# Second stage: another order for the work before the first scores, one output column and one product of v exchanged, two output columns begun in the tail

## The chip, the cores and the metric

The kernel runs on one core of a Trainium2 chip. The metric is the device time of one execution in microseconds; the number of the kernel before is the median of three runs.

## The reference

Three layers in a row on 8 batches of 576 tokens and 512 features (8 heads of 64): attention with keys and values averaged in groups of 8, a gated MLP with a product over the tokens, and a layer of four experts. The second stage of the kernel is the last one:

```python
logits = x @ w_gate
topk = np.argpartition(-logits, K, axis=-1)[..., :K]      # K = 2
...
for e in range(E):                                        # E = 4
    q = x @ wq[e]
    k = x @ wk[e]
    v = x @ wv[e]
    scores = scale * (q @ k.transpose(0, 2, 1))
    scores = np.where(causal, -1000000000.0, scores)
    scores = scores - scores.max(-1, keepdims=True)
    a = np.exp(scores)
    a /= a.sum(-1, keepdims=True) + 1e-09
    ye = a @ v @ wo[e]
    for kk in range(K):
        mask = topk[:, :, kk] == e
        out += mask[..., None] * w[:, :, kk:kk + 1] * ye
```

## The kernel before

The first stage (attention and MLP, until about 589 us) writes its result to DRAM as two parts, a high one of TensorE's precision and the remainder. Class PhaseB is the second stage. Every product of fp32 accuracy is made of three matmuls on such parts: high by high, high by low, low by high.

The four experts are two pairs p. For a batch b and a pair p there are nine units u, each a tile of scores: QT lists them as (row of 128 tokens i, expert of the pair e), and e = 2 is the last 64 tokens of both experts together. The main loop in run goes over all 8 x 2 x 9 units in this order, and in its step k issues:

- score of unit k: matmuls on TensorE (PE, L827 to L840), mask and maximum on VectorE (DVE, L832, L834, L841), the exponential on ScalarE (ACT, L844);
- scale of unit k - 1: sum and reciprocal on DVE (L855, L856), the scaling of the probabilities pr on GpSimd (POOL, L860), or on DVE for the units in SDF (batch 0) and SDL (last batch);
- the fill items of that step (below);
- after units 5 and 8, av: the product of probabilities and v of one expert (PE L906, ACT L910, DVE L911, then the parts ah and al, ACT L916 and DVE L917);
- trans of unit k - 3 (LAG): the transposes of pr (PE L873, L886) and their two parts pbh and pbl (ACT L877, L890, DVE L882, L891).

So the order of each engine's work is the order in which the program issues it, and the tables of fill items set where the rest goes. An item of two characters is: xN, load chunk N of the next batch's input; 1N, part N of the projections of this batch's pair 1 (0 and 1 are q's halves, 2 and 3 k's halves, 12 matmuls each); 0N, the same of the next batch's pair 0; vN, product of v for the next batch, tokens N; g, the next batch's gates; oN, output column N of the batch before (12 matmuls L928 to L930, two evictions on ACT L931, one transfer L932). FIRSTF, FILL and LASTF are the tables of batch 0, of batches 1 to 6 and of the last one; PRE is issued ahead of the first unit, for batch 0 itself.

A half of k is copied on ACT (L744, tile scr), its remainder taken on DVE (L745), and after the second half four transfers spread it (kd, L751, on SP's queue). q goes the same way (ACT L726, L728, L734, DVE L729, L731, two transfers qz, L737). v is copied at L785. All products go through a ring of 8 PSUM banks (bank); outp's tile o has 3 buffers. The last batch's output columns come behind the main loop, which runs LAG + 1 = 4 steps past the last unit.

Of the kernel before, what the change touches and what calls it, by code (L numbers as in the profile page):

```python
# [8 lines left out]
F32 = mybir.dt.float32  # L9
# [7 lines left out]
B, H, S, D = 8, 8, 576, 64  # L17
# [24 lines left out]
class PhaseA:  # L42


    def __init__(self, ctx, tc, w, ins, x2d):
        self.tc, self.nc, self.ins, self.x2d = tc, tc.nc, ins, x2d
        self.c = self.w = w
        self.ps = ctx.enter_context(tc.tile_pool(name="a_ps", bufs=1, space=bass.MemoryType.PSUM))
        self.E, self.LN, self.XX, self.XU, self.GG = {}, {}, {}, {}, {}
        self.P, self.X32, self.XH, self.XL, self.U, self.G = {}, {}, {}, {}, {}, {}  # L50
        self.PT, self.VN, self.QT, self.KV, self.RAW, self.STG = {}, {}, {}, {}, {}, {}
# [396 lines left out]
    def outp(self, b, f):  # L448
        nc, w = self.nc, self.w
        ps = self.ps.tile([128, 2, 512], F32, tag="mm", name="op", bufs=2)  # L450
        c = slice(f * 128, f * 128 + 128)
        for h in range(2):
            s = slice(h * HS, h * HS + HS)
            o = ps[:, h, :HS]
            for k in range(4):
                gh, gl = self.G[b, k]
                nc.tensor.matmul(o, self.wo[0][:, k, c], gh[:, s], start=k == 0, stop=False)  # L457
                nc.tensor.matmul(o, self.wo[0][:, k, c], gl[:, s], start=False, stop=False)  # L458
                nc.tensor.matmul(o, self.wo[1][:, k, c], gh[:, s], start=False, stop=k == 3)  # L459
        hi, lo = (w.tile([128, 2, HS], F32R, tag="x2", name=n, bufs=4) for n in ("x2h", "x2l"))  # L460
        x = ps[:, :, :HS] if f < 3 else lo.bitcast(F32)
        nc.vector.tensor_add(x, ps[:, :, :HS], self.X32.pop((b, f)))
        nc.scalar.activation(hi, x, AF.Copy)  # L463
        (nc.vector if f < 3 else nc.gpsimd).tensor_sub(lo, x, hi.bitcast(F32))  # L464
        for i, t in enumerate((hi, lo)):
            nc.sync.dma_start(self.x2d[b][:, f, i], t.bitcast(F32).rearrange("p a b -> p (a b)"))

    def run(self):
        self.weight_tiles()
        for b in range(B):  # L470
            n = b + 1
            more = n < B
            if b == 0:
                self.first()
            else:
                self.middle(b)
            if n + 1 < B:
                self.load_k(n + 1)
                self.load_v(n + 1, 0)
                self.load_q(n + 1)  # L480
            ahead = 1 if b else 0
            for f in range(4):
                if more:
                    if f == 0:
                        self.finish(n, 4)
                    self.trans(n, f + ahead)
                self.outp(b, f)
            if more:
                if not ahead:
                    self.trans(n, 4)  # L490
                self.av(n, (2, "r", 0, 1, 3))
# [121 lines left out]
LAG = 3  # L613
ALV = 1
KDM = 1
FILL = (('', '12 10 11', '', '13 x0 x1 x2 x3', '', '', 'o3 o1 o0', '', ''), ('v0', 'v1 00 02', '01 o2', '03', '', '', '', 'v2 v3', 'v4 g'))
FIRSTF = (('10', '11', '12', '13 x0 x1 x2 x3', '', '', '', '', ''), ('v0 00', '', '01 02 v1', '03', '', '', '', 'v2 v3', 'v4 g'))
LASTF = (('', '10 12 11', '', '', '13', '', 'o1', '', 'o0'), ('', '', '', '', '', 'o2', '', '', 'o3'))
SDF = {(0, 0), (0, 1), (0, 5), (0, 8), (1, 0), (1, 2), (1, 7)}
SDL = {(0, 4), (0, 6), (1, 6), (1, 7)}  # L620
PRE = 'v0 00 01 02 03 v1 v2 v3 v4 g'
AVS = [(0, 256), (256, S)]


class PhaseB:


    def __init__(self, ctx, tc, w, ins, x2d, out, ident):
        self.tc, self.nc, self.ins, self.x2d, self.out, self.ident = tc, tc.nc, ins, x2d, out, ident
        self.c = self.w = w  # L630
        self.ps = ctx.enter_context(tc.tile_pool(name="b_ps", bufs=1, space=bass.MemoryType.PSUM))
        self.X, self.QK, self.V, self.GW, self.U, self.PT, self.AV, self.AH = {}, {}, {}, {}, {}, {}, {}, {}

    def load_x(self, b, kc):
        nc, w = self.nc, self.w
# [280 lines left out]
            nc.scalar.activation(ah[:, lo:up], a[:, lo:up], AF.Copy)  # L916
            (nc.vector if ALV else nc.gpsimd).tensor_sub(al[:, lo:up], a[:, lo:up], ah[:, lo:up].bitcast(F32))  # L917

    def outp(self, b, f):
        nc, w = self.nc, self.w  # L920
        c = slice(128 * f, 128 * f + 128)
        o = w.tile([128, S], F32, tag="vg", name="o", bufs=3)
        for lo, up in AVS:
            ps = self.bank("op")[:, :up - lo]
            s = slice(lo, up)
            for p in range(2):
                ah, al = self.AH[b, p]
                nc.tensor.matmul(ps, self.wo[0][:, p, c], ah[:, s], start=p == 0, stop=False)  # L928
                nc.tensor.matmul(ps, self.wo[1][:, p, c], ah[:, s], start=False, stop=False)
                nc.tensor.matmul(ps, self.wo[0][:, p, c], al[:, s], start=False, stop=p == 1)  # L930
            nc.scalar.activation(o[:, s], ps, AF.Copy)  # L931
        nc.sync.dma_start(self.out[b, :, f], o)  # L932

    def run(self):
        self.consts()
        for kc in range(4):
            self.load_x(0, kc)
        self.weights()
        part = lambda b, p: [lambda w=w, h=h: self.proj(b, w, p, h) for w in "qk" for h in range(2)]
        vpart = lambda b: [lambda t=t: self.vproj(b, t) for t in range(NT)]  # L940
        units = [(b, p, u) for b in range(B) for p in range(2) for u in range(9)]
        def item(b, x):
            if x[0] == "x":
                return [lambda: self.load_x(b + 1, int(x[1]))] if b + 1 < B else []
            if x[0] == "o":
                return [lambda: self.outp(b - 1, int(x[1]))] if b > 0 else []
            if x[0] == "1":
                return [part(b, 1)[int(x[1])]]
            if b + 1 == B:
                return []  # L950
            if x[0] == "0":
                return [part(b + 1, 0)[int(x[1])]]
            if x[0] == "v":
                return [vpart(b + 1)[int(x[1])]]
            return [lambda: self.gate(b + 1)]
        for x in PRE.split():
            for f in item(0 if x[0] == "1" else -1, x):
                f()
        for k in range(len(units) + LAG + 1):
            if k < len(units):  # L960
                b, p, u = units[k]
                self.score(b, p, u)
            if 0 <= k - 1 < len(units):
                self.scale(*units[k - 1])
            if k < len(units):
                for x in (LASTF if b + 1 == B else FILL if b else FIRSTF)[p][u].split():
                    for f in item(b, x):
                        f()
            j = k - LAG
            if 0 <= j - 1 < len(units):  # L970
                b_, p_, u_ = units[j - 1]
                if u_ in (5, 8):
                    for g in range(2):
                        self.av(b_, p_, u_ // 8, g)
            if 0 <= j < len(units):
                self.trans(*units[j])
        for f in range(4):
            self.outp(B - 1, f)


def host_b(inputs, a):
# [34 lines left out]
```

## Time and profile before

| | |
|---|---|
| time, median of 3 runs (lowest, highest) | 969.14 us (969.02, 970.92) |
| the profiled execution: time, span | 967.84 us, 966.1 us |
| mean granted clock of TensorE | 0.982 |
| busy: PE, DVE, ACT, POOL | 95%, 72%, 54%, 46% |

Times in the rows are microseconds from the start of the span. A row of the timeline is one instruction or a few of a kind: start, duration, engine, line and operation, output <- inputs, shapes, and in brackets the time for which the engine had been idle, with what the profile takes to have released it. Matmuls overlap, so their durations add up to more than the time they take; the distance of their starts tells it.

### The profile page before, as it was taken

How to read it: one execution, taken by the hardware profiler on the slowest of the kernel's cores; microseconds unless marked ns; L12 is line 12 of the kernel's file. 1: busy time of each engine (PE TensorE's matmuls, PEld its weight loads, DVE VectorE, ACT ScalarE, POOL GpSimd, SP SyncE). 2: the span in 40 equal slices, each digit the busy share in tenths (PEclk: the TensorE clock that was granted, in tenths of full speed). 3: DMA queues.
4: the chain of work that ended last, by engine and by line, in shares of the span. 5: the costliest groups of instructions: out<-in, count | busy, mean ns of one | idle time of the engine just before them, and what ended most of it. 6: DMA issues, size and time to landing. Idle time of an engine off the chain costs nothing.

```text
span 966.1 us, 18451 instructions
## 1 busy us (share of the span) xinstructions
PE 915.0 (95%) x6488; PEld 864.4 (89%) x6488; DVE 693.1 (72%) x1869; ACT 519.0 (54%) x1285; POOL 447.0 (46%) x628
## 2 busy tenths in 40 slices
PE   4887699999999999999999999899999999999997
PEld 3677689989989999899899899799999999999987
DVE  6998557757667577577576514897878796878785
ACT  3755334344343343343443433677777777777776
POOL 6545847558369368376583560113222222323221
PEclk9797899999999999999999999999999999999999
DMA  9611522312402404223126014415253534435121
GB/s 326 236 35 44 172 80 82 121 61 71 157 25 81 160 13 140 99 65 132 56 61 191 25 39 134 140 37 176 61 172 88 162 94 147 118 108 163 49 61 75
DMA packets 51644, 102.86 MB, mean 106 GB/s; under 512 B 10592, under 2 KB 16736, under 8 KB 50656
## 3 DMA queue, kind: packets, MB, share of 16 engines
q1 hardware_dynamic: 51408, 101.68, 32.9%
q8 instruction: 52, 0.85, 0.4%
q14 instruction: 40, 0.33, 0.1%
q10 hardware_dynamic: 144, 0.00, 0.0%
HBM read 59.72 MB, written 28.31 MB: 91 GB/s over the span
## 4 chain that ended last, share of the span: by engine, by line
PE 63%; DVE 20%; ACT 6%; POOL 5%; issue 3%; DMA 2%; SPq 1%; POOLq 0%; ACTq 0%; DVEq 0%
PE av L906 4%; PE op L457 4%; PE op L458 4%; PE op L459 3%; PE sp L434 3%; PE sp L432 3%; PE sp L433 3%; PE sc L224 3%; PE t L886 3%; DVE vnl L402 3%; PE pj L715 2%; PE pj L713 2%; PE pj L714 2%; DVE vnh L404 2%; DVE bs L388 2%
## 5 line engine op out<-in xcount | busy, mean ns | idle before, releaser
L860 POOL TENSOR_SCALAR pr<-pr,sm,gw 128x128 f32<-128x128 f32 (+3 forms) x119 | 72.7, 612 | 208.1 <-DVE sm L856 140.9
L844 ACT ACTIVATE pr<-s,sm 128x256 f32<-128x256 f32 (+4 forms) x160 | 83.2, 521 | 41.6 <-DVE sm L841 18.0
L432 PE MATMUL sp<-wsh,vnh 128*128 128x288 f32 x256 | 78.8, 309 | 5.0 <-ACT vnh L400 5.0
L458 PE MATMUL op<-g,woh 128*128 128x288 f32 x256 | 77.0, 301 | 6.8 <-POOL g L445 6.8
L457 PE MATMUL op<-g,woh 128*128 128x288 f32 x256 | 78.5, 309 | 0.3 <-DVE x2l L464 0.3
L416 PE MATMUL up<-x,wih 128*128 128x288 f32 x256 | 76.8, 300 | 1.5 <-ACT xu L324 1.5
L433 PE MATMUL sp<-wsh,vnl 128*128 128x288 f32 x256 | 77.0, 301 | 0.0
L434 PE MATMUL sp<-wsl,vnh 128*128 128x288 f32 x256 | 76.6, 299 | 0.0
L418 PE MATMUL up<-x,wil 128*128 128x288 f32 x256 | 75.7, 296 | 0.0
L715 PE MATMUL pj<-xbh,wql 128*128 128x288 f32 x256 | 75.5, 295 | 0.0
L713 PE MATMUL pj<-xbh,wqh 128*128 128x288 f32 x256 | 75.5, 295 | 0.0
L714 PE MATMUL pj<-xbl,wqh 128*128 128x288 f32 x256 | 75.5, 295 | 0.0
L459 PE MATMUL op<-g,wol 128*128 128x288 f32 x256 | 75.3, 299 | 0.0
L417 PE MATMUL up<-x,wih 128*128 128x288 f32 x256 | 75.1, 293 | 0.0
L841 DVE CUSTOM_DVE_ANT_0 s<-s,mk 128x512 f32<-128x512 f32 (+3 forms) x128 | 62.4, 487 | 3.5 <-PE t L886 2.9
L224 PE MATMUL sc<-kbd,qt 128*128 128x144 f32 (+1 forms) x320 | 50.8, 306 | 14.2 <-DMA qt<-q_in 8.4
L891 DVE TENSOR_TENSOR pbl<-t,pbh 128x512 fp32r<-128x512 f32 (+3 forms) x128 | 60.7, 484 | 3.4 <-ACT pbh L890 1.7
L886 PE MATMUL t<-ident,pr 128*128 128x128 f32 x320 | 57.7, 280 | 4.8 <-POOL pr L860 2.6
L224 PEld LDWEIGHTS sc<-kbd,qt 128*128 128x128 f32 (+1 forms) x320 | 44.4, 192 | 18.3 <-issue 11.1
L906 PE MATMUL av<-pbh,vt 128*128 128x320 f32 (+4 forms) x224 | 55.6, 278 | 2.4 <-ACT pbh L890 2.4
L400 ACT ACTIVATE vnh<-vg,rs 128x512 fp32r<-128x512 f32 (+1 forms) x40 | 27.3, 717 | 54.9 <-POOL rs L392 43.0
L464 POOL TENSOR_TENSOR x2l<-x2l,x2h 128x576 fp32r<-128x576 f32 x8 | 11.4, 1430 | 97.1 <-ACT x2h L463 97.1
(247 smaller groups left out, 3352.8 us busy)
## 6 DMA issues: line engine op xcount, KB each, us to landing
kraw<-k_in SPq DMA_DIRECT2D x16, 576.0 KB, 3.8
x<-x2h SPq DMA_DIRECT2D x32, 288.0 KB, 2.1
x<-x2l SPq DMA_DIRECT2D x32, 288.0 KB, 2.1
xbl<-x SPq DMA_DIRECT2D x32, 288.0 KB, 4.1
xbh<-x SPq DMA_DIRECT2D x32, 288.0 KB, 4.0
kd<-scr SPq DMA_DIRECT2D x64, 144.0 KB, 2.5
out<-o SPq DMA_DIRECT2D x32, 288.0 KB, 3.7
vraw<-v_in SPq DMA_DIRECT2D x16, 512.0 KB, 4.3
```

What stands on the lines that cost most here:

```text
L224: nc.tensor.matmul(ps[:m, p // 2, (p % 2) * 144:(p % 2) * 144 + 144], qt[:, p, o:o + m], kbd[:, p, :], start=p % 2 == 0, stop=True, skip_g ...
L432: nc.tensor.matmul(o, vh[:, k, c], self.ws[0][:, k, s], start=k == 0, stop=False)
L433: nc.tensor.matmul(o, vl[:, k, c], self.ws[0][:, k, s], start=False, stop=False)
L434: nc.tensor.matmul(o, vh[:, k, c], self.ws[1][:, k, s], start=False, stop=False)
L457: nc.tensor.matmul(o, self.wo[0][:, k, c], gh[:, s], start=k == 0, stop=False)
L458: nc.tensor.matmul(o, self.wo[0][:, k, c], gl[:, s], start=False, stop=False)
L459: nc.tensor.matmul(o, self.wo[1][:, k, c], gh[:, s], start=False, stop=k == 3)
L713: nc.tensor.matmul(ps, self.wq[0][:, kc, c], xh[:, s], start=kc == 0, stop=False)
L714: nc.tensor.matmul(ps, self.wq[0][:, kc, c], xl[:, s], start=False, stop=False)
L715: nc.tensor.matmul(ps, self.wq[1][:, kc, c], xh[:, s], start=False, stop=kc == 3)
L886: nc.tensor.transpose(ps[:, j], pt[:, 128 * j:128 * j + 128], self.ident)
L906: nc.tensor.matmul(ps[:, s - lo:], vt[:, j, 2 * p + e].rearrange("p a d -> p (a d)"), t[:, e, j * PTS + s:j * PTS + up], start=j == 0 and ...
```

## The change

Three tables and one function change. PRE issues v's products and the gates first, then k, then q, then q of pair 1 (items 10 and 11), which leaves FIRSTF; 12 goes one unit earlier there. In FILL, o0 moves from unit 6 of pair 0 to unit 0 of pair 1, v0 from unit 0 to unit 1, and 02 from unit 1 to unit 2, in front of 01. A new table TAILF issues, in the second and the fourth of the four steps behind the last unit, the first six matmuls of output columns 0 and 1 of the last batch, those of pair 0 (two banks each, kept in self.OP); the six of pair 1, the evictions and the transfer follow behind the loop.

```diff
-FILL = (('', '12 10 11', '', '13 x0 x1 x2 x3', '', '', 'o3 o1 o0', '', ''), ('v0', 'v1 00 02', '01 o2', '03', '', '', '', 'v2 v3', 'v4 g'))
-FIRSTF = (('10', '11', '12', '13 x0 x1 x2 x3', '', '', '', '', ''), ('v0 00', '', '01 02 v1', '03', '', '', '', 'v2 v3', 'v4 g'))
+FILL = (('', '12 10 11', '', '13 x0 x1 x2 x3', '', '', 'o3 o1', '', ''), ('o0', 'v0 v1 00', '02 01 o2', '03', '', '', '', 'v2 v3', 'v4 g'))
+FIRSTF = (('', '12', '', '13 x0 x1 x2 x3', '', '', '', '', ''), ('v0 00', '', '01 02 v1', '03', '', '', '', 'v2 v3', 'v4 g'))
+TAILF = ('', 'i0', '', 'i1')
...
-PRE = 'v0 00 01 02 03 v1 v2 v3 v4 g'
+PRE = 'v0 v1 v2 v3 v4 g 02 03 00 01 10 11'
...
-    def outp(self, b, f):
+    def outp(self, b, f, pair=None):
...
-        o = w.tile([128, S], F32, tag="vg", name="o", bufs=3)
-        for lo, up in AVS:
-            ps = self.bank("op")[:, :up - lo]
+        first = pair == 0
+        o = None if first else w.tile([128, S], F32, tag="vg", name="o", bufs=3)
+        for i, (lo, up) in enumerate(AVS):
+            if first or pair is None:
+                self.OP[f, i] = self.bank("op")[:, :up - lo]
+            ps = self.OP[f, i]
             s = slice(lo, up)
-            for p in range(2):
+            for p in range(2) if pair is None else (pair,):
...
+            if first:
+                continue
             nc.scalar.activation(o[:, s], ps, AF.Copy)
-        nc.sync.dma_start(self.out[b, :, f], o)
+        if not first:
+            nc.sync.dma_start(self.out[b, :, f], o)
...
+            else:
+                for x in TAILF[k - len(units)].split():
+                    self.outp(B - 1, int(x[1]), 0)
...
         for f in range(4):
-            self.outp(B - 1, f)
+            self.outp(B - 1, f, 1 if f < 2 else None)
```

How the order moves is shown at three places. The first is ACT's queue in batch 1, from unit 6 of pair 0 on; o<-op are the evictions of output columns, two for each. Before:

```order
L931 ACTIVATE o<-op 128x256
L844 ACTIVATE pr,sm<-s,sm 128x512
L931 ACTIVATE o<-op 128x320
L931 ACTIVATE o<-op 128x256
L844 ACTIVATE pr,sm<-s,sm 128x384
L931 ACTIVATE o<-op 128x320
L931 ACTIVATE o<-op 128x256
L931 ACTIVATE o<-op 128x320
L890 ACTIVATE pbh<-t 128x2x128
L890 ACTIVATE pbh<-t 128x128
L844 ACTIVATE pr,sm<-s,sm 128x256
L890 ACTIVATE pbh<-t 128x4x128
```

After the change (line numbers are up by one, in outp by six):

```order
L937 ACTIVATE o<-op 128x256
L845 ACTIVATE pr,sm<-s,sm 128x512
L937 ACTIVATE o<-op 128x320
L937 ACTIVATE o<-op 128x256
L845 ACTIVATE pr,sm<-s,sm 128x384
L937 ACTIVATE o<-op 128x320
L891 ACTIVATE pbh<-t 128x2x128
L891 ACTIVATE pbh<-t 128x128
L845 ACTIVATE pr,sm<-s,sm 128x256
L891 ACTIVATE pbh<-t 128x4x128
L845 ACTIVATE pr,sm<-s,sm 128x128
L937 ACTIVATE o<-op 128x256
```

Two of the six evictions are gone from between the exponentials, and those of o0 stand behind the units' transposes.

The second place is ACT's queue at the start of stage 2, around the first exponentials (pr,sm<-s); qs and scr are the copies of q and k. Before:

```order
L774 ACTIVATE vt_6025<-vs 128x4x64
L844 ACT_TABLE_LOAD
L844 ACTIVATE pr,sm<-s_6248,sm 128x320
L798 ACTIVATE gg<-gg 128x20
L844 ACTIVATE pr,sm<-s_6252,sm 128x256
L726 ACTIVATE qs_6011<-pj 64x288
L728 ACTIVATE qs_6011<-pj 64x288
L844 ACTIVATE pr,sm<-s,sm 128x512
```

After the change:

```order
L729 ACTIVATE qs_6011<-pj 64x224
L729 ACTIVATE qs_6011<-pj 64x64
L735 ACTIVATE qs_6011<-pj 64x64 x2
L745 ACTIVATE scr<-pj 128x288
L845 ACTIVATE pr,sm<-s,sm 128x512
L845 ACTIVATE pr,sm<-s_6288,sm 128x320
L845 ACTIVATE pr,sm<-s_6292,sm 128x256
L845 ACTIVATE pr,sm<-s,sm 128x384
```

The copies of q of pair 1 and the first of its k now stand ahead of the first exponential; before they stood between the exponentials and behind them. The table load has moved up to the gates' exponential.

The third place is PE's queue in the tail, from the end of the next to last av. Before:

```order
L906 MATMUL av<-pbh,vt_6026 128x64
L886 MATMUL t<-ident,pr 128x128 x6
L906 MATMUL av<-pbh,vt_6026 128x256
L906 MATMUL av<-pbh,vt_6026 128x320
L906 MATMUL av<-pbl,vt_6026 128x320
```

After the change:

```order
L907 MATMUL av<-pbh,vt_6026 128x64
L887 MATMUL t<-ident,pr 128x128 x3
L932 MATMUL op<-ah,wqh 128x256
L933 MATMUL op<-ah,wql 128x256
L934 MATMUL op<-al,wqh 128x256
L932 MATMUL op<-ah,wqh 128x320
L933 MATMUL op<-ah,wql 128x320
L934 MATMUL op<-al,wqh 128x320
L887 MATMUL t<-ident,pr 128x128 x3
```

The six transposes of the last three units, in one piece before, now stand in two threes, with six matmuls of an output column behind each.

## Rows read from the trace of the kernel before

**Rows 1.** The page: span, and busy time of PE and PEld among the engines.

```profile
span 966.1 us, 18451 instructions
...
PE 915.0 (95%) x6488; PEld 864.4 (89%) x6488; DVE 693.1 (72%) x1869; ACT 519.0 (54%) x1285; POOL 447.0 (46%) x628
```

**Rows 2.** Windows: stretch, length, busy PE, PEld, DVE, ACT, POOL; granted clock, DMA share, GB/s.

```profile
680.80:708.80 28.00, 27.86 (x216) 27.18 (x216) 24.84 (x100) 21.96 (x69) 7.83 (x13) 1.00 0.43 112
708.80:725.80 17.00, 17.00 (x133) 16.74 (x132) 11.60 (x46) 11.63 (x38) 4.21 (x7) 1.00 0.40 135
...
658.40:663.20 4.80, 4.80 (x38) 4.71 (x37) 4.66 (x16) 3.75 (x13) 0.45 (x1) 1.00 0.92 267
...
640.00:920.00 280.00, 278.83 (x2155) 273.60 (x2154) 227.62 (x921) 209.36 (x660) 76.00 (x119) 1.00 0.40 116
...
619.30:622.70 3.40, 3.08 (x14) 3.11 (x15) 2.12 (x12) 1.32 (x5) 1.20 (x2) 0.50 0.99 346
```

**Rows 3.** Timeline, PE, batch 1, pair 0, unit 6: output products and the transposes behind.

```profile
659.17 0.28 PE L928 MATMUL op<-ah,wqh 128*128 128x256 f32 x1
...
663.83 0.31 PE L930 MATMUL op<-al,wqh 128*128 128x320 f32 x1
...
664.43 0.27 PE L886 MATMUL t<-ident,pr 128*128 128x128 f32 x1
...
664.72 0.62 PE L886 MATMUL t<-ident,pr 128*128 128x128 f32 x4
```

**Rows 4.** Timeline there: POOL's scaling of units 4 and 5, VectorE's reciprocal, the exponential.

```profile
662.63 0.45 POOL L860 TENSOR_SCALAR pr<-pr,sm,gw 128x128 f32<-128x128 f32 x1 [4.76 <-DVE sm L856]
663.40 0.78 POOL L860 TENSOR_SCALAR pr<-pr,sm,gw 128x512 f32<-128x512 f32 x1 [0.32 <-ACT o L931]
...
663.04 0.17 DVE L856 RECIPROCAL sm<-sm 128x1 f32<-128x1 f32 x1
...
661.94 0.69 ACT L844 ACTIVATE pr<-s,sm 128x512 f32<-128x512 f32 x1 [1.05 <-DVE sm L855]
```

**Rows 5.** Timeline, the same place in batch 6: PE's transposes of unit 5, POOL's scaling.

```profile
890.25 0.62 PE L886 MATMUL t<-ident,pr 128*128 128x128 f32 x4
...
888.92 0.77 POOL L860 TENSOR_SCALAR pr<-pr,sm,gw 128x512 f32<-128x512 f32 x1 [0.32 <-ACT o L931]
```

**Rows 6.** Timeline, VectorE at fill item 03 of batch 1.

```profile
680.82 0.46 DVE L745 TENSOR_TENSOR qs<-pj,scr 128x288 fp32r<-128x288 f32 x1 [0.33 <-ACT scr L744]
```

**Rows 7.** Timeline, PE at the start of stage 2: the first and last of six waits.

```profile
611.42 0.74 PE L873 MATMUL t<-ident,pr 128*128 128x128 f32 x5 [0.23 <-DVE pr L860]
...
619.62 1.09 PE L886 MATMUL t<-ident,pr 128*128 128x128 f32 x4 [1.45 <-DVE sm L855]
```

**Rows 8.** Timeline at the start: ACT, DVE, SP's queue; page, kd (KB each, us to landing).

```profile
604.73 1.28 ACT L844 ACT_TABLE_LOAD   x1
606.02 0.53 ACT L844 ACTIVATE pr<-s,sm 128x320 f32<-128x320 f32 x1
...
610.70 0.58 DVE L860 TENSOR_SCALAR pr<-pr,sm,wl 128x576 f32<-128x576 f32 x1
...
598.17 2.38 SPq L751 DMA_DIRECT2D kd<-scr  x4
...
kd<-scr SPq DMA_DIRECT2D x64, 144.0 KB, 2.5
```

**Rows 9.** Timeline, PE in batch 4: a product of v waits for its input.

```profile
802.76 0.39 PE L782 MATMUL vp<-wqh,xbl 128*128 128x260 f32 x1 [0.33 <-DMA xbl<-x]
```

**Rows 10.** Timeline of the tail: last av, last product (PE); the copies of ah (ACT).

```profile
953.86 0.53 PE L906 MATMUL av<-pbh,vt 128*128 128x256 f32 x2 [0.78 <-ACT pbh L890]
...
962.21 0.31 PE L930 MATMUL op<-al,wqh 128*128 128x320 f32 x1
...
956.33 0.89 ACT L916 ACTIVATE ah<-scr 128x256 fp32r<-128x256 f32 x2
```

**Rows 11.** Window of the tail, columns as in rows 2.

```profile
950.00:966.10 16.10, 11.66 (x86) 10.90 (x85) 6.08 (x20) 8.57 (x25) 0.45 (x1) 1.00 0.25 93
```

More of the change, by code (lines that the diff above doesn't have):

```diff
@@ L631, in __init__ @@
         self.ps = ctx.enter_context(tc.tile_pool(name="b_ps", bufs=1, space=bass.MemoryType.PSUM))
-        self.X, self.QK, self.V, self.GW, self.U, self.PT, self.AV, self.AH = {}, {}, {}, {}, {}, {}, {}, {}
+        self.X, self.QK, self.V, self.GW, self.U, self.PT, self.AV, self.AH, self.OP = {}, {}, {}, {}, {}, {}, {}, {}, {}
     def load_x(self, b, kc):
```

## The prediction

> **What bounds the kernel.** I read the page first: TensorE (PE) is busy 915.0 of 966.1 us [rows 1], so outside the joints of the program the time is PE's work, and a reordering can only win or lose PE's idle time. The profiled execution took 967.84 us, 1.74 more than its span; the three runs have a median of 969.14, 1.30 above it. All sums below are made against 967.84, and 1.30 is added at the end. A measurement of this kernel can tell about 0.2% (1.9 us) from no change.
>
> Next I read the windows of stage 2. A batch has two halves. From k's second half (fill item 03) to the transposes of unit 5 of the next pair 0, both PE (27.86 of 28.00 us) and VectorE (24.84, no single idle piece over 0.5) have hardly any room [rows 2]; its last part, 658.40 to 663.20, has VectorE busy 4.66 of 4.80. From there to the next 03, 17 us, PE is busy 17.00 and VectorE only 11.60, so that half is PE's alone [rows 2]. Over batches 1 to 6 and some more, 640 to 920, PE is busy all but 1.2 us [rows 2]. What idle time there is lies at stage 2's start and in the last batch. So the question for each edit is: into which half does it put PE's work?
>
> **The column that changes halves (FILL).** Before, o3 o1 o0 are 36 matmuls that run from 659.17 to the last one's start at 663.83 [rows 3]: 4.66 / 35 = 0.133 us each, so column o0 is 12 x 0.133 = 1.60 us of PE. The change takes it out of unit 6 of pair 0 and puts it at unit 0 of pair 1, behind unit 5's transposes; v0 goes one unit later, which leaves PE's sum there as it was. o0's evictions go along, and its output transfer starts later, with nobody waiting for it.
>
> What stands behind o0 on PE? The transposes of units 4 and 5, which read probabilities that POOL has scaled. POOL finishes unit 4 at 662.63 + 0.45 = 663.08 and unit 5 at 663.40 + 0.78 = 664.18 [rows 4]; PE reads them at 664.43 and 664.72 [rows 3]. So PE comes 1.35 and 0.54 us after them. POOL's last scaling waits for VectorE's reciprocal at 663.04 + 0.17 [rows 4], the end of the stretch in which VectorE is full [rows 2], and nothing in that chain reads the output product. Batch 6 looks the same: 888.92 + 0.77 = 889.69 against 890.25, 0.56 [rows 5]. With o0 gone PE arrives 1.60 earlier, finds unit 5 not ready and stands for 1.60 - 0.54 = 1.06 us (some 0.3 of it already at unit 4). The 1.60 us then come back in the half where PE has no idle time, and by the time of item 03, where VectorE idles 0.33 and so is level with PE again [rows 6], nothing has made it good. Six batches use this table: **+6.4 us**. The ends: 0, if unit 5 gets ready earlier by as much; 9.6 (6 x 1.60), if the slack of 0.54 is gone too. I take 6.4, since slack and chain read alike in batches 1 and 6.
>
> **The start (PRE, FIRSTF).** Same matmuls, another order: v and gates, k, q, and the next pair's q now come before the first score. Before, PE has six idle pieces from 611.42 to 619.62, summing to 4.35 us, each in front of transposes whose probabilities are late (the first and the last stand in [rows 7]); then follow 3.4 us at granted clock 0.50 with PE busy 3.08 [rows 2], which cost half of that, 1.5. Those 5.9 are all that can be won. By the new order PE reaches the end of item 13 as before, near 611.1, but the first exponentials now queue on ScalarE behind the copy of item 12. I followed the chain by hand: 12 leaves PE near 608.7, its copy takes 0.4; three exponentials follow (0.53 for 320 columns [rows 8], in proportion for 512 and 256), to about 611.2; VectorE's reciprocal, its backlog of k's remainders and the scaling (0.58 [rows 8]) bring unit 0's transposes to about 612.9, later than 611.42. From there fewer copies stand between, q's being over, and I come to 617.5 for unit 4 and 618.7 for unit 5, against 619.62. So most of the idle moves to the front instead of going away: **-0.9**. The ends: -5.9, and +1.5, the delay of unit 0, if nothing behind it is made up. I take -0.9 because the row nearest to it, unit 5's, is at the end of the same chain.
>
> On SP's queue the four copies of k now come ahead of q's two. Four are issued in 2.38 us, so the last one 1.8 after the first, and land 2.5 after their issue [rows 8]: 4.3 us. By the new order k's second half leaves ScalarE near 600.7, so its copies are there near 605.0. The first score is to start near 606.0, so about 1 us covers them; if that cover is gone, the score waits for the excess. ScalarE's table load (1.28 us [rows 8]) now stands between k's two copies. The Trainium skill's page "ScalarE: Activation LUTs", section "What ACT_TABLE_LOAD costs", counts a drain of about 1.38 us on top of a load of 1.28; the row shows the load with the first exponential right behind it at 606.02, so the trace gives no such drain as a cost. By that rule k's copies would land 0.4 after the score wants them, and the start would come to about -0.5 instead of -0.9.
>
> **One wait for input (v0 later).** In batch 4 v's products wait 0.33 us for the low half of the next input [rows 9]. They now come 1.6 us later: **-0.3**. The ends are 0 and -0.3.
>
> **The tail (TAILF).** The first six matmuls of two columns (12, 1.60 us) go among the last transposes, where PE waits 0.78 us for ScalarE's copy [rows 10]. The last attention product then starts about 0.6 later; but the rest, 36 products instead of 48, soon needs the new ah, whose two copies end 0.9 us after 956.33 on ScalarE [rows 10] and now sit 0.6 later, with two output evictions ahead of the last piece. PE waits some 1.1 us there. So 1.60 comes off behind, 0.6 is added before and about 0.6 net of what was idle anyway behind: **-0.4**, last product near 961.8 instead of 962.21 [rows 10]. The ends: -1.6 (all of it), +0.6 (none).
>
> **Sum.** +6.4 - 0.9 - 0.3 - 0.4 = +4.8: 967.84 + 4.8 = 972.6 for a profiled execution, and 972.6 + 1.3 = **973.9 us** for the median.
>
> **Rival 1: the gap doesn't arise (not slower).** ScalarE loses o0's two evictions from this half, and if the exponential of unit 5 had stood behind an output eviction, unit 5 would be ready earlier. For it: evictions and exponentials take turns in that queue. Against it: that exponential began at 661.94 after 1.05 us of idle, waiting for VectorE [rows 4]. It decides from the point where unit 5 is ready 1.06 us earlier; then the term is 0 and the sum -0.9 - 0.3 - 0.4 = -1.6, or 967.5, and faster beyond doubt as soon as the start gives 0.3 more. Chance 0.18, of it 0.10 faster and 0.08 within the measurement.
>
> **Rival 2: the start's idle goes whole.** If unit 0's exponentials come in front of the backlog and the queue behind it stays clear, PE never waits for probabilities and the clock does not fall: -5.9 instead of -0.9, so 973.9 - 5.0 = 968.9. For it: q's copies, which stood between exponentials, are over. Against it: item 12 ahead of the first exponential. Chance 0.12: 0.04 faster, 0.05 within, 0.03 slower, by what the FILL gap comes to.
>
> **Rival 3: the new gap takes the clock along.** At the start the idle pieces of up to 1.45 us [rows 7] were followed by the stretch at 0.50 [rows 2], a loss of about 1.5. Were each of the six gaps followed by one, it would be 6 x 1.5 = 9 more: 982.9. Against it: at 953.86 PE idled 0.78 and the clock stayed at 1.00 [rows 10, 11]; the new gaps would be single too, those at the start were six. The Trainium skill's page "TensorE: Matmul & The Clock Gate", section "A second HAM failure mode: psum-queue depth-cycling", tells of a kernel whose TensorE idled briefly between groups of matmuls and whose clock swung between its levels; the start agrees with it, the gap at 953.86 doesn't. Chance 0.06.
>
> **The numbers.** The forecast has the rest, 0.64, all of it slower; its own range is 971 to 977: the start's middle values and the tail's ends around 973.9. Faster is 0.10 + 0.04 = 0.14, within 0.2% 0.08 + 0.05 = 0.13, slower 0.64 + 0.03 + 0.06 = 0.73. The range goes from 966.5, which takes in rival 2 and most of rival 1, to 977.5, the forecast with its start at +1.5 and its tail at +0.6 and a unit for the slack; rival 3 and the far ends of the others, under 0.2, lie outside.
>
> **What would show it.** In the changed kernel: PE idle of 0.2 to 0.4 us ahead of unit 4's transposes and 0.7 to 0.9 ahead of unit 5's in each of batches 1 to 6, released by POOL, with the clock at 1.00; the period of a batch 1.06 us longer; the wait for the low input half gone; at the start unit 0's transposes near 612.9 and unit 5's near 618.7; the last product 0.4 us earlier against the last batch's start. If PE has no idle ahead of unit 5's transposes, the main term is wrong; if the gap is there but a batch is no longer than before, my claim that the other half is PE's alone is wrong; if the idle pieces at the start are gone, rival 2 holds.

## The result and the profile after

| | before | after |
|---|---|---|
| median (lowest, highest) | 969.14 us (968.5, 970.92), 5 runs | 974.34 us (972.83, 975.16), 5 runs |
| the profiled execution: time, span | 967.84, 966.1 | 972.83, 971.0 |
| PE busy | 915.0 us, 95% | 917.3 us, 94% |

The ratio is 1.0053, with a 95% interval of 1.0039 to 1.0067: slower, by 5.2 us. The forecast was 973.9 for the median and 972.6 for the profiled execution.

Single executions of either kernel differ by some 2 us, and part of that lies in the first stage: the second one began between 588.97 and 591.78 us in the profiles taken. So the second stage is read from points on PE's timeline: its first product, unit 5's transposes of pair 0 in a batch, the last output product, and the span's end. In the profile after, PE's timeline has these points, and the waits of the start and of a batch:

```profile
589.98 0.36 PE L782 MATMUL vp<-wqh,xbh 128*128 128x260 f32 x1 [0.90 <-issue]
612.93 0.73 PE L874 MATMUL t<-ident,pr 128*128 128x128 f32 x5 [1.50 <-DVE sm L856]
617.89 0.33 PE L887 MATMUL t<-ident,pr 128*128 128x128 f32 x1 [1.98 <-POOL pr L861]
619.09 0.63 PE L887 MATMUL t<-ident,pr 128*128 128x128 f32 x4 [0.70 <-DVE pr L861]
...
658.33 0.28 PE L932 MATMUL op<-ah,wqh 128*128 128x256 f32 x1
...
661.87 0.28 PE L841 MATMUL s<-qs,qzvlo 128*128 128x256 f32 x1
662.28 0.33 PE L887 MATMUL t<-ident,pr 128*128 128x128 f32 x1
...
662.51 0.28 PE L841 MATMUL s<-qs,qzvlo 128*128 128x128 f32 x1
663.37 0.66 PE L887 MATMUL t<-ident,pr 128*128 128x128 f32 x4 [0.58 <-POOL pr L861]
...
893.47 0.66 PE L887 MATMUL t<-ident,pr 128*128 128x128 f32 x4 [0.58 <-POOL pr L861]
...
966.57 0.31 PE L934 MATMUL op<-al,wqh 128*128 128x320 f32 x1
```

The first row is stage 2's start, the next three are the waits of the start [rows 7], then come the first output product of batch 1, the transposes of units 4 and 5 there with the score products ahead of them, unit 5's transposes in batch 6 [rows 3, 5], and the last output product [rows 10]. Of before, stage 2's start and the score products ahead of the transposes of units 4 and 5:

```profile
589.70 0.36 PE L781 MATMUL vp<-wqh,xbh 128*128 128x260 f32 x1 [0.90 <-issue]
...
664.32 0.28 PE L840 MATMUL s<-qs,qzvlo 128*128 128x256 f32 x1
664.60 0.28 PE L840 MATMUL s<-qs,qzvlo 128*128 128x128 f32 x1
```

From these and the rows of before:

| stretch | before | after | difference |
|---|---|---|---|
| stage 2's start to unit 5, batch 0 | 29.92 | 29.11 | -0.81 |
| from there to the first output product of batch 1 | 39.55 | 39.24 | -0.31 |
| from there to unit 5, batch 1 | 5.55 | 5.04 | -0.51 |
| unit 5, batch 1 to batch 6 | 225.53 | 230.10 | +4.57 |
| unit 5, batch 6, to the last output product | 71.96 | 73.10 | +1.14 |
| from there to the end of the span | 3.89 | 4.43 | +0.54 |

The fifth stretch holds the sixth batch's column, 1.60, less 0.46 gained in the tail. The sum is 4.62 in stage 2; stage 1 took 0.28 longer, and together they are the span's 4.9.

The gap stands where the prediction put it. POOL's timeline in batch 1 (compare [rows 4]), with VectorE's last reciprocal of that chain:

```profile
661.78 0.45 POOL L861 TENSOR_SCALAR pr<-pr,sm,gw 128x128 f32<-128x128 f32 x1 [4.77 <-DVE sm L857]
662.55 0.77 POOL L861 TENSOR_SCALAR pr<-pr,sm,gw 128x512 f32<-128x512 f32 x1 [0.32 <-ACT o L937]
...
662.19 0.16 DVE L857 RECIPROCAL sm<-sm 128x1 f32<-128x1 f32 x1
```

Unit 5's probabilities are ready at 662.55 + 0.77 = 663.32, and PE reads them 0.05 later, at 663.37; before it came 0.54 later [rows 3, 4]. Unit 4's are ready at 662.23, and PE reads them at 662.28. The reciprocal comes 662.19 - 658.33 = 3.86 us after the first output product; before it was 663.04 - 659.17 = 3.87. Against the first output product the chain did not move; only PE came earlier and stood. (The brackets put the wait of POOL's second scaling down to ScalarE's o. The scaling reads no o, and in both kernels it begins 0.19 to 0.20 behind the end of that reciprocal, at 663.21 before and 662.35 after.) The waits of PE over batches 1 to 6, by what it waited for (us in total, times, longest), after and then before:

```profile
PE t L887 <- POOL pr L861: 3.5, 6, 0.6
```

```profile
PE av L906 <- DVE pbl L891: 0.5, 3, 0.2
PE vp L782 <- DMA xbl<-x: 0.3, 1, 0.3
```

Six waits, one in each batch, have taken the place of the four small ones. The windows show the same as busy time (columns as in [rows 2]):

```profile
640.00:920.00 280.00, 274.98 (x2110) 268.24 (x2110) 222.81 (x900) 206.73 (x647) 73.73 (x116) 1.00 0.39 116
...
663.40:681.00 17.60, 17.60 (x136) 17.50 (x137) 11.31 (x45) 11.61 (x37) 4.03 (x7) 1.00 0.37 121
...
619.90:623.30 3.40, 3.40 (x17) 3.40 (x16) 2.20 (x9) 1.88 (x7) 1.04 (x2) 0.50 0.78 257
```

PE idles 5.0 us where it idled 1.2, which is 3.8 more and less than the batches grew. The brackets and the windows count a matmul as busy until its modelled end, and matmuls overlap, so a break costs more than they show. By the distance of starts, unit 4's transposes come 662.28 - 661.87 = 0.41 behind the score product ahead of them, where before it was 664.43 - 664.32 = 0.11, and unit 5's 663.37 - 662.51 = 0.86, where it was 664.72 - 664.60 = 0.12: 0.30 + 0.74 = 1.04 us lost in this batch. The half behind unit 5 is PE's from end to end; the clock stays at 1.00 through the new gaps, and the stretch at 0.50 behind the start is still there [rows 2].

### The profile page after: what moved, and what is told of

Same layout as the page of the kernel before. It is cut to its first block, busy times and chain, and to the rows that moved or that the text cites. A ratio compares the mean times of both kernels' runs of the same rounds, so it can differ in the third digit from the quotient of the medians.

```text
span 971.0 us, 18440 instructions
## 1 busy us (share of the span) xinstructions
PE 917.3 (94%) x6488; PEld 866.7 (89%) x6488; DVE 694.9 (72%) x1869; ACT 519.7 (54%) x1285; POOL 446.5 (46%) x628
## 4 chain that ended last, share of the span: by engine, by line
PE 55%; DVE 26%; ACT 8%; POOL 5%; issue 4%; DMA 1%; SPq 0%; ACTq 0%; POOLq 0%; DVEq 0%
PE op L457 4%; PE op L458 4%; PE sc L224 3%; PE op L459 3%; PE sp L434 3%; PE sp L433 3%; PE sp L432 3%; DVE s L842 3%; ACT pr L845 3%; DVE vnl L402 3%; PE av L907 3%; DVE pbl L892 2%; DVE vnh L404 2%; DVE bs L388 2%; PE tr L275 2%
```

## The experiments

Each kernel is the one before with the edit shown, unless said otherwise. "A batch" is a fifth of the time from unit 5 of batch 1 to unit 5 of batch 6 in its profile.

**The table of batches 1 to 6 alone**

```diff
-FILL = (... 'o3 o1 o0' ...), ('v0', 'v1 00 02', '01 o2', ...
+FILL = (... 'o3 o1' ...), ('o0', 'v0 v1 00', '02 01 o2', ...
```

> Only the table of batches 1 to 6 is changed; start and tail are as before. Theory: the whole loss is here. Each of six batches gains 1.60 us of PE work in the half that is PE's alone and loses only the 0.5 us of slack ahead of unit 5's transposes, so 6 x 1.1 = 6.5, less the 0.33 us wait for input and some 0.5 us of small waits that were there before: 5.7 over the kernel before, about 974.8. Rival: the loss comes from start or tail, or from the three edits together; then this is within 1 us of the kernel before.

Measured: 974.56 us against 968.95, ratio 1.0061 (1.0047 to 1.0076): 5.6 more, where 5.7 was expected. A batch took 46.08. The loss is in this table.

**The start alone**

```diff
-PRE = 'v0 00 01 02 03 v1 v2 v3 v4 g'
+PRE = 'v0 v1 v2 v3 v4 g 02 03 00 01 10 11'
-FIRSTF = (('10', '11', '12', '13 x0 x1 x2 x3', ...
+FIRSTF = (('', '12', '', '13 x0 x1 x2 x3', ...
```

> Only the order ahead of stage 2 and the table of batch 0 are changed. Theory: the idle pieces move from six places to three and the half-clock stretch stays, so 1.1 us less than the kernel before, about 968.0. Rival: without the other edits the idle goes whole, 5.9 less; or it costs what batch 0 pays later, no gain at all.

Measured: 968.28 against 968.95, ratio 0.9998 (0.9987 to 1.0009). The times alone can't tell a gain of 1.1 from none; they exclude 5.9. In its profile PE has the three waits of the kernel after, and unit 5 of batch 0 comes 620.71 - 591.60 = 29.11 us after stage 2's start, 0.81 earlier than before:

```profile
614.55 0.74 PE L873 MATMUL t<-ident,pr 128*128 128x128 f32 x5 [1.51 <-DVE sm L855]
619.50 0.33 PE L886 MATMUL t<-ident,pr 128*128 128x128 f32 x1 [1.98 <-POOL pr L860]
620.71 0.63 PE L886 MATMUL t<-ident,pr 128*128 128x128 f32 x4 [0.69 <-DVE pr L860]
```

**The tail alone**

```diff
+TAILF = ('', 'i0', '', 'i1')
```

with outp and the end of run as in the change.

> Only the tail is changed. Theory: the last product comes 0.46 us earlier, but the fourth column's eviction waits for the first column's transfer to free its tile and the end behind the last product is 0.54 longer: 0.1 more than before, about 969.2. Rival (my prediction's own term): 0.4 less, about 968.7, with no wait of ScalarE for a transfer of the output.

Measured: 968.87 against 968.95, ratio 0.9998 (0.9986 to 1.001): no difference, as the theory says, though the rival's 0.4 could not be told from it by the times. The profile tells: the last product comes 71.50 us after unit 5 of batch 6 instead of 71.96, and the end 4.43 behind it instead of 3.89. ScalarE's last evictions wait for the transfer of an earlier output column:

```profile
962.39 1.17 ACT L937 ACTIVATE o<-op 128x320 f32<-128x320 f32 x3 [0.81 <-PE op L934]
965.06 0.71 ACT L937 ACTIVATE o<-op 128x256 f32<-128x256 f32 x2 [1.50 <-DMA out<-o]
```

**Column o0 alone**

```diff
-FILL = (... 'o3 o1 o0' ...), ('v0', ...
+FILL = (... 'o3 o1' ...), ('o0 v0', ...
```

> On the kernel before, only column o0 moves from unit 6 of pair 0 to unit 0 of pair 1; v0 and 02 stay where they were. Theory: o0 alone makes the loss, 6 x 1.09 = 6.5 with the wait for input still there: about 975.7, PE waiting for POOL's scaling ahead of the transposes of units 4 and 5 in each batch. Rival: the moves of v0 and 02 make it; then this is within 1 us of the kernel before.

Measured: 974.52 against 968.95, ratio 1.006 (1.0047 to 1.0073): 5.6 more, where 6.5 was expected. A batch took 46.02, each of the five between 45.99 and 46.04, the same as in the kernel after. The theory holds. Its surcharge for the wait for input is not borne out, though the interval (4.6 to 7.1) doesn't exclude it: PE waits for no input over batches 1 to 6 in this profile, and o0 in front of v0 puts v0 off by itself.

**v0 and 02 alone, o0 left where it was**

```diff
-FILL = ... ('v0', 'v1 00 02', '01 o2', ...
+FILL = ... ('', 'v0 v1 00', '02 01 o2', ...
```

> On the kernel before, o0 stays at unit 6 of pair 0; only v0 goes one unit later and 02 behind it in front of 01. Theory: no PE work changes halves, so no loss; every batch takes 44.9 us, since v's first product no longer waits for the low half of the input, which cost 0 to 1.5 us in some batches in the profiles of kernels with v0 early (1.0 to 2.5 us in five batches): 1 to 2 us less than the kernel before, about 967.5. Rival: the input waits are just met later, or the moves cost something themselves: 969 or more.

Measured: 967.18 against 969.04, ratio 0.9981 (0.9971 to 0.999): 1.9 less. A batch took 44.94, and none of the five more than 45.00; before they took 44.90 to 45.68, and in the profile of the start alone, where v0 is early too, one took 46.40. PE's waits over batches 1 to 6 in the profile of the start alone:

```profile
PE vp L782 <- DMA xbl<-x: 0.6, 2, 0.3
PE vp L781 <- DMA xbh<-x: 0.6, 1, 0.6
PE av L906 <- DVE pbl L891: 0.5, 3, 0.2
```

With v0 later the two lines on the input are gone. More profiles say the same. Over five batches the four kernels with v0 early and o0 in place (before, the start alone, the tail alone, the tail with one more tile) took 1.0, 2.5, 2.2 and 2.3 us more than 5 x 44.9; this one and the two further down with v0 later took 224.53 to 224.68, 0.2 more at most.

**Two columns moved**

```diff
-FILL = (... 'o3 o1 o0' ...), ('v0', ...
+FILL = (... 'o3' ...), ('o0 o1 v0', ...
```

> On the kernel before, o0 and o1 both move from unit 6 of pair 0 to unit 0 of pair 1. Theory: the slack of 0.5 us is used up by the first, so the second column costs its full 1.60 us of PE time in each of six batches: a batch of 44.9 + 1.1 + 1.6 = 47.6 us, 6 x 2.7 = 16.3 more than before, about 985. Rival: with fewer evictions in ScalarE's queue the chain to unit 5's probabilities gets shorter, and the second column costs less than half of that: under 980.

Measured: 986.5 against 969.04, ratio 1.0179 (1.0162 to 1.0195): 17.5 more. From the second on a batch took 47.81 to 47.85: 1.8 more for the second column, a little over its 1.60 of PE's time. There is no relief from fewer evictions: in batch 1 unit 5's probabilities are ready 663.13 + 0.77 - 658.70 = 5.20 us behind the first output product, where it was 4.99 in the kernel after. The scaling, and the waits, which are those expected:

```profile
663.13 0.77 POOL L860 TENSOR_SCALAR pr<-pr,sm,gw 128x512 f32<-128x512 f32 x1 [0.53 <-PE t L886]
...
PE t L886 <- POOL pr L860: 15.2, 12, 1.7
```

**The opposite move: o2 into the half that waits**

```diff
-FILL = (... 'o3 o1 o0' ...), (..., '01 o2', ...
+FILL = (... 'o3 o1 o0 o2' ...), (..., '01', ...
```

> On the kernel before, the opposite move: o2 goes from unit 2 of pair 1 into unit 6 of pair 0, behind o0. Theory: PE has no idle there to fill, and the other half then has 1.6 us less of PE work; the probabilities wait for PE instead of PE for them, with VectorE's slack in the other half (3 us and more) to take it: a batch stays at 44.9 to 45.1, about 969. Rival: the two halves are balanced, and any move costs as much as o0's: 974 or more.

Measured: 972.21 against 969.04, ratio 1.0036 (1.0024 to 1.0048): 3.2 more, between theory (0) and rival (5 or more), and so against the theory. A batch took 45.74, 0.8 more than the 44.9 without waits. No long wait is behind it. PE's timeline behind item 03 (its av begins at 680.42 here, at 680.18 before):

```profile
680.83 0.30 PE L906 MATMUL av<-pbh,vt 128*128 128x320 f32 x1
681.17 0.38 PE L906 MATMUL av<-pbl,vt 128*128 128x256 f32 x1
...
684.69 0.38 PE L886 MATMUL t<-ident,pr 128*128 128x128 f32 x2
684.93 0.39 PE L839 MATMUL s<-kd,qs 128*128 128x256 f32 x1
685.15 0.28 PE L840 MATMUL s<-qs,qzgln 128*128 128x256 f32 x1
685.27 0.28 PE L781 MATMUL vp<-wqh,xbh 128*128 128x260 f32 x1
```

The step from 680.83 to 681.17 is 0.34, more than twice the 0.15 from one such product to the next, and the score follows the transposes after 0.24 where it took 0.13 before (684.15 to 684.28). From av to the first product of v it is 685.27 - 680.42 = 4.85 us instead of 684.61 - 680.18 = 4.43. So 0.42 of the 0.8 comes back in two pieces behind item 03, where PE, with 1.60 us less to do in its half, arrives early. For the first piece the profile names VectorE's remainders pbl (five waits of at most 0.2 over batches 1 to 6, 1.0 in all); what the score waited for, and where the other 0.4 of a batch lies, was not traced.

**The tail with one more tile**

```diff
+        if pair == 1 and f == 0:
+            o = w.tile([128, 640], F32R, tag="P", name="o5", bufs=5)[:, :S].bitcast(F32)
+        else:
+            o = None if first else w.tile([128, S], F32, tag="vg", name="o", bufs=3)
```

on the tail alone; the ring "P" holds the input chunks, of which the last batch uses four.

> The tail's change alone, as in the run of the tail, with the first column's result in a free buffer of the input ring instead of the ring of three output tiles. Theory: the fourth column's evictions no longer wait for the first column's transfer, so the end behind the last product is 3.9 us again instead of 4.43 while the last product stays 0.46 earlier: 0.5 less than the run of the tail, about 968.4. Rival: something else holds that eviction, and the end stays at 4.4.

Measured: 968.43 against 969.04, ratio 0.9997 (0.9986 to 1.0008). By the times that is no difference, and the 0.5 expected can't be told from none. In the profile the last product comes after 71.48 us and the end 3.91 behind it, as expected; the last evictions wait for PE alone:

```profile
961.89 0.39 ACT L940 ACTIVATE o<-op 128x256 f32<-128x256 f32 x1 [0.33 <-PE op L937]
962.74 0.44 ACT L940 ACTIVATE o<-op 128x320 f32<-128x320 f32 x1 [0.46 <-PE op L937]
```

**The parts that gained, together**

The change with this FILL and the tail's extra tile:

```diff
-FILL = (... 'o3 o1' ...), ('o0', 'v0 v1 00', '02 01 o2', ...
+FILL = (... 'o3 o1 o0' ...), ('', 'v0 v1 00', '02 01 o2', ...
```

> The parts that gained, together: the new start, v0 later with o0 left at unit 6 of pair 0, the tail with the first column's result in a free buffer of the input ring. Theory: the gains are in different places and add up: 1.9 (v0 later, as measured) + 1.1 (start) + 0.5 (tail) = 3.5 less than the kernel before, about 965.5. Rival: the start's gain is given back before the first full batch, and v0's gain alone remains: about 967.

Measured: 966.71 against 968.86, ratio 0.9976 (0.9965 to 0.9987): 2.2 less than before, and so some 7.4 less than after (5.2 + 2.2). That is nearer to the rival's 967 than to the 965.5 of the sum. In the profiled execution, one of the slower at 969.12, unit 5 of batch 0 (29.12), a batch (44.91) and the tail (71.45 and 3.83) are all as the theory has them; what it lost lies in batch 0, where pair 1's first scores waited for the copies of k and the half clock lasted 6.83 us instead of 3.40:

```profile
621.09 0.55 PE L828 MATMUL s<-kd,qs 128*128 128x320 f32 x1 [0.18 <-DMA kd<-scr]
622.16 0.61 PE L829 MATMUL s<-kd,qs 128*128 128x320 f32 x1 [0.53 <-DMA kd<-scr]
...
621.14:627.97 6.83, 6.30 (x26) 5.99 (x27) 3.20 (x12) 1.82 (x7) 0.99 (x2) 0.50 0.42 124
```

From unit 5 of batch 0 to unit 5 of batch 1 this profile took 47.21 us, where the next run, with the same order on PE, took 44.80. The kernel after had no such wait. Whether this happens in most executions is not shown; one profile of this kernel was taken.

**Two scalings less for VectorE at the start**, on the kernel of the run before this one

```diff
-SDF = {(0, 0), (0, 1), (0, 5), (0, 8), (1, 0), (1, 2), (1, 7)}
+SDF = {(0, 5), (0, 8), (1, 0), (1, 2), (1, 7)}
```

> The run of the parts together, with the scaling of units 0 and 1 of batch 0 on POOL instead of VectorE. Theory: PE's three waits at the start hang on VectorE, which is 90% busy there; two scalings of 0.58 and 0.54 us off it bring units 4 and 5 up to 1.1 us earlier, at the price of some 0.3 at unit 0: 0.8 less than the run it is compared with. Rival: POOL's scaling of unit 0 (0.8 us) and its later start hold unit 0's transposes, and everything behind shifts with them: no gain, or 0.3 more.

Measured: 966.01 against 968.86, ratio 0.9972 (0.9963 to 0.9981). The rival holds for the start: unit 5 of batch 0 comes 619.51 - 590.04 = 29.47 us after stage 2's start, 0.35 later than without the edit, with all three waits still there:

```profile
613.18 0.77 PE L874 MATMUL t<-ident,pr 128*128 128x128 f32 x5 [1.70 <-POOL pr L861]
618.30 0.33 PE L887 MATMUL t<-ident,pr 128*128 128x128 f32 x1 [2.12 <-POOL pr L861]
619.51 0.63 PE L887 MATMUL t<-ident,pr 128*128 128x128 f32 x4 [0.69 <-DVE pr L861]
```

Its median is 0.7 lower than the last one's with intervals that overlap; in its profile batch 0 had no wait for k. Both kernels are faster than the two that were compared.

## Why the prediction was right

**The column that changes halves.** Right in mechanism, place and size. Predicted were 1.06 us of gap in a batch and six of them, 6.4. Measured: batches of 46.02 against 44.9 where no input wait lengthens them, 1.12 each, 6.7 for six. The slack of 0.54 went down to 0.05 and not to 0, and that is most of the difference. Of the two gaps that were to show it, 0.2 to 0.4 and 0.7 to 0.9, the brackets give only 0.58 for the second; by the distance of starts both are there, 0.30 and 0.74. The column alone gives the whole loss (5.6), a second column the whole of its own time, and the chain to unit 5's probabilities stayed where it was, 3.86 and 3.87 us behind the first output product. With that rival 1 is out: no gain from fewer evictions was seen with one column, nor with two. One reading of the prediction is not right: VectorE does have an idle piece over 0.5 in the half that it called full, at its very end. It lies behind unit 5's reciprocal, and no term rests on it:

```profile
708.80 0.15 DVE L855 TENSOR_SCALAR sm<-sm 128x1 f32<-128x1 f32 x1 [0.71 <-ACT pr L844]
```

**The start.** Predicted -0.9, with unit 0's transposes at 612.9, unit 4's at 617.5 and unit 5's at 618.7. They came at 612.93, 617.89 and 619.09, with stage 2 beginning 0.28 later; the gain is 0.81 at that point and 1.1 by batch 1's first output product. The idle went from 4.35 in six pieces to 1.50 + 1.98 + 0.70 = 4.18 in three: it moved, as said. That is 0.17 of the 0.81; the other 0.64 lies in time that the profile counts as PE's work, 29.92 - 4.35 = 25.57 us before and 29.11 - 4.18 = 24.93 after, for the same matmuls. Three breaks fewer, each dearer than its bracket as above, fit that; how much of it is theirs was not tried. Rival 2 is out. ScalarE's table load stood between k's two copies, right behind the first (598.58 + 0.39 = 598.97) and with its next instruction 1.30 us after its own start:

```profile
598.58 0.39 ACT L745 ACTIVATE scr<-pj 128x288 fp32r<-128x288 f32 x1
598.99 1.28 ACT L799 ACT_TABLE_LOAD   x1
600.29 0.22 ACT L799 ACTIVATE gg<-gg 128x20 f32<-128x20 f32 x1
600.41 0.39 ACT L745 ACTIVATE scr<-pj 128x288 fp32r<-128x288 f32 x1
```

No first score waited for k in this profile. The drain that the Trainium skill counts on top of the load ("ScalarE: Activation LUTs", section "What ACT_TABLE_LOAD costs") did not show as a cost here either.

**One wait for input.** This term was mis-sized, and its ends, 0 and -0.3, were read from a single execution. The wait differs between executions: 1.0 us over five batches in the profile of before, 2.5 in that of the start alone (226.99 against 5 x 44.9), 2.2 and 2.3 in two more. Moving v0 alone gained 1.9 (1.0 to 2.8).

**The tail.** Predicted -0.4. The last product did come 0.46 earlier, and by the parts that were priced: the last av starts 959.26 - 955.78 = 3.48 us behind the one before it, where it was 953.86 - 950.98 = 2.88, so 0.60 later, and from there to the last product it is 7.31 instead of 8.35:

```profile
955.78 0.36 PE L907 MATMUL av<-pbh,vt 128*128 128x320 f32 x1
959.26 0.43 PE L907 MATMUL av<-pbh,vt 128*128 128x256 f32 x2
...
950.98 0.36 PE L906 MATMUL av<-pbh,vt 128*128 128x320 f32 x1
```

(The last row is of before.) But the sum stopped there. Behind it the end took 0.54 longer: four output columns share three tiles, the order of PE's products made the columns' evictions finish in a bunch, and the fourth column waited for the first one's transfer. So the step that failed is the one that valued the tail by the last product alone and named no resource behind it. An extra tile took the 0.54 back in its profile (3.91 us of end).

**Rival 3.** The clock stayed at 1.00 through gaps of 0.58 us (0.86 by the distance of starts), as the row at 953.86 had suggested [rows 10, 11].

The two misses, +0.5 at the end and -0.7 or more on the input, have opposite signs, and the sum came within 0.44 us of the median partly for that reason: that closeness is luck. The profiled execution lay 0.2 above its forecast; stage 1, which the change doesn't touch, alone took 0.28 longer in it.

## What to carry to other kernels

Where an engine is 95% busy, find the stretches in which another engine is only just ahead of it, and those in which it alone is busy all the time. In this kernel, work moved from the first into the second cost its full time less that small lead, each time round, and a move the other way was not free either. A measure of slack, the time from a result being ready to its being read, gives the size before any run: here 0.54 us of slack against 1.60 us of work. Follow an edit past the last instruction that it moves, to the tiles and transfers behind, and take a wait for a transfer from more than one execution.

## What was not expected of the hardware

With two columns moved, the half clock did follow PE's longer gaps in one batch of six. In each batch PE waited 1.74 us and then 0.79; in batch 1 a stretch at 0.50 began in the second wait (first window), while the same place of the next batch, with the same two waits, stayed at 1.00 (second window):

```profile
663.30:666.70 3.40, 2.75 (x12) 2.75 (x13) 2.02 (x11) 1.70 (x8) 2.22 (x4) 0.50 0.86 290
...
708.00:714.90 6.90, 4.37 (x35) 4.02 (x34) 6.15 (x27) 4.96 (x17) 2.84 (x5) 1.00 1.00 301
```

What set the two apart was not tried. And one kernel's executions differ by 2 to 5 us; a part of that lies in waits for input in the middle of the program: batches of 44.9 to 46.4 us with the same instructions in the same order.
